# A fused adaLN attention + MLP block, forward and backward: TensorE and the SP queue in one written order, K kept on chip in the first chunk, memsets moved off GpSimd

One core of a Trainium2 chip. The metric is device time of one execution in microseconds (us), slowest core, and here there is only one. A program on one core runs "fast" or shows itself by being over 1.5% longer than the fastest run of the same kernel.

## The reference, cut to what matters

```python
def _fwd_reference(A_x, A_wqkv, A_wo, B_x, B_w1, B_b1, B_w2, B_b2, c, w_mod):   # S=2048, D=512, H=32, Dh=16, F=1792
    mod = (_silu(c) @ w_mod).reshape(c.shape[0], 6, 1, -1)
    sa, ca, ga, sb, cb, gb = ...                          # six rows of mod
    h = _layernorm(x) * (1 + ca) + sa                     # LN1
    x = x + ga * attention(h, A_wqkv, A_wo)               # softmax over all 2048 keys, 32 heads of 16
    h = _layernorm(x) * (1 + cb) + sb                     # LN2
    x = x + gb * (relu(h @ w1 + b1) ** 2 @ w2 + b2)
    return x

def reference(..., grad_out):
    out, vjp = jax.vjp(_f, ...)                           # gradients of x, weights, biases, c, w_mod
    return (out, *vjp(grad_out))
```

Ten outputs in bfloat16: the block's output and nine gradients.

## The kernel before

The program runs through these stages: an opening (LN1, first K, Q and V), forward attention over four query chunks of 512 (each 8 groups of 4 heads, two head pairs a group, 16 key blocks a pair: 256 exponential tiles a chunk), with other work woven in between as a "background" of generators; the last chunk's MLP with the weight gradients dW1 and dW2; the attention backward (16 head pairs, 16 slots of 4 tiles each); a tail. Short names: PV is the product of the exponentials with V, dS the gradient of the scores, which one DMA transpose a slot turns for the product that follows. In chunk 0 the background is the K, Q and V projections, in later chunks the MLP of the chunk before.

A scheduler places the instructions of each engine's queue, unless an engine is named in `manual_schedule`: then that engine's instructions stay in the order in which the program text emits them ("written order"). In the kernel before only TensorE is so named, in three regions. The SP engine here issues DMAs alone: loads, stores and DMA transposes.

```python
        def load_k(g):                                   # K of a group: back from DRAM
            t = kp.tile([P, S], BF16, name="KTq")
            nc.gpsimd.dma_start(t[:], self.KTq_d[g])
            return t
...
        with tc.manual_schedule(engines={mybir.EngineType.PE}):
            first = self.gen_open(Vaug, KT, QTm, stp)
            next(first)
            for n, (qc, g, jp) in enumerate(order):
                if (qc, g, jp) == (1, 0, 0):
                    bg.drain()                           # all that is left of Q, K, V is emitted here
                    self.close_qkv()
                    self.open_mlp()
                    bg.add(self.gen_weights())
...
    def gen_open(self, Vaug, KT, QTm, stp):              # (cut)
        for s4 in range(0, ST, 4):
            nc.sync.dma_start(x0[:, s4:s4 + 4, :], x_v[:, s4:s4 + 4, :])
        for t in (1, 0):
            nc.gpsimd.memset(wpads[t][:], 0.0)
...
            if s4 == 0:                                  # at the end of LN1's first block
                nc.gpsimd.dma_start(self.wmod[:, :, 2 * D:6 * D], wmod_v[:, :, 2 * D:6 * D])
...
    def gen_qkv(self):                                   # (cut) background of chunk 0
        for g in range(1, NQ):
            for s0 in range(0, S, 512):
                yield from self.gen_fm(self.mps, 1, g, s0)       # K
            yield from self.gen_fm(self.mps, 0, g, 0)            # Q of chunk 0
            yield (g, 0)
        for g in range(NQ):
            for s0 in range(512, S, 512):
                yield from self.gen_fm(self.mps, 0, g, s0)       # Q of the other chunks
        for s0 in range(0, ST, 4):                               # V transposed, for the backward
            vT = self.qkv_eb.tile([P, NQ, 4 * P], BF16, name="vT", bufs=1)
            for k in range(4):
                vp = self.vpads[k % 2]
                ...                                              # two GpSimd copies into vp
                nc.sync.dma_start_transpose(vT[:, :, k * P:(k + 1) * P], vp[:].rearrange("p g j e -> p (g j e)"))
            nc.gpsimd.dma_start(self.VTq_d.rearrange("g p s -> p g s")[:, :, s0 * P:(s0 + 4) * P], vT[:])
            yield 0
...
    def gen_weights(self):                               # (cut) background at the start of chunk 1
        nc.sync.dma_start(wo[:], ...)
        nc.sync.dma_start(w1[:], ...)
        nc.sync.dma_start(w2[:], ...)
        nc.sync.dma_start(b1r[:], ...)
        ...
        nc.sync.dma_start_transpose(self.wogaT[:] ..., wo[:] ...)
        yield ("wait", 8)
        pb = self.mps.tile([P, 1024], BF16, name="pps")
        nc.tensor.transpose(pb[:, :FT], b1r[:], self.ident[:FT, :FT])     # TensorE meets b1 here
        ...
        nc.sync.dma_start_transpose(self.W1mT[:] ..., w1[:] ...)
        nc.sync.dma_start_transpose(self.W2gbT[:] ..., w2[:] ...)
...
    def gen_mlp(self, sc, O_b):                          # (cut) comes after gen_weights in the background
        nc.sync.dma_start_transpose(OT[:] ..., O_b[:] ...)
        nc.sync.dma_start_transpose(gT[:], io["grad_out"][0, s0:s0 + 512, :])
        yield ("wait", 7)
        ...                                              # wo product, LN2
        nc.sync.dma_start_transpose(xhT[:] ..., xh[:] ...)
...
    def attn_bwd(self):                                  # (cut) one slot = G = 4 tiles
                        for c in range(SC):
                            for ib0 in range(0, ST, G):
                                if pieces and (c or ib0):
                                    nc.sync.dma_start(*pieces.pop(0))     # loads of the next group / pair
                                ...                                        # 4 tiles: scores, exp, dP, dS
                                nc.sync.dma_start_transpose(dsT[:], dsg[:].rearrange("p i a k -> p (i a k)"))
```

`pair_pieces` and `load_group` make 15 loads a group, 2.9 MB: four of 0.5 MB together during its first pair (for its own second pair), eleven of 2.4 MB during its second (for the next group). Each dS transpose moves 128 x 4096 bfloat16 numbers, 1 MB.

The softmax here doesn't subtract the row's maximum and nothing guards it: scores larger than these inputs give would overflow.

## Time and profile before

| stretch of the profiled run | length, us | what it is |
|---|---|---|
| start to first exponential | 56.5 | LN1, first K, Q, V |
| forward chunk 0 | 296.1 | attention, Q/K/V projections beside it |
| forward chunk 1 | 247.5 | attention, weights and MLP of chunk 0 beside it |
| forward chunk 2 | 250.3 | attention, MLP of chunk 1 |
| forward chunk 3, to its last exponential | 249.5 | attention, MLP of chunk 2 |
| to first exponential of the backward | 220.5 | last MLP chunk, dW1, dW2 |
| backward, first to last exponential | 1484.0 | |
| tail | 190.9 | |

The chunk borders are the starts of the 257th, 513th and 769th forward exponential. 1024 exponentials of 0.934 us make 239 us a chunk, so what a chunk takes beyond 239 is ScalarE standing. The median of three runs was 2989.28 us (2985.57 to 2990.15). The lines of the profile are in the prediction.

### The profile page before, as it was taken

How to read it: one execution, taken by the hardware profiler on the slowest of the kernel's cores; microseconds unless marked ns; L12 is line 12 of the kernel's file. 1: busy time of each engine (PE TensorE's matmuls, PEld its weight loads, DVE VectorE, ACT ScalarE, POOL GpSimd, SP SyncE). 2: the span in 40 equal slices, each digit the busy share in tenths (PEclk: the TensorE clock that was granted, in tenths of full speed). 3: DMA queues.
4: the chain of work that ended last, by engine and by line, in shares of the span. 5: the costliest groups of instructions: out<-in, count | busy, mean ns of one | idle time of the engine just before them, and what ended most of it. 6: DMA issues, size and time to landing. Idle time of an engine off the chain costs nothing. (4 is left out here: it accounts for less than half of the span.)

```text
span 2995.3 us, 72543 instructions
## 1 busy us (share of the span) xinstructions
PE 2714.6 (91%) x29931; PEld 1413.4 (47%) x30431; DVE 1799.5 (60%) x2728; ACT 2245.3 (75%) x3380; POOL 368.3 (12%) x617
## 2 busy tenths in 40 slices
PE   4699889999999988799999999999999999999796
PEld 2355445545555544744444444444444444444343
DVE  5222223322322244658888888888888888888475
ACT  3599999999999974227777777777777777777443
POOL 6233211210221132340000000000000000000000
PEclk9899999999999999999999999999999999999898
DMA  6645722330431257979999999999999999999942
GB/s 176 170 115 130 150 51 85 94 92 20 126 96 42 90 151 165 201 161 191 186 209 189 205 194 191 205 191 201 199 188 208 187 204 198 187 191 179 223 136 62
DMA packets 1304924, 467.13 MB, mean 156 GB/s; under 512 B 1235310, under 2 KB 1268592, under 8 KB 1304592
## 3 DMA queue, kind: packets, MB, share of 16 engines
q1 hardware_dynamic: 1274256, 374.68, 67.4%
q0 software_dynamic: 28224, 85.16, 9.7%
q8 instruction: 238, 3.90, 0.5%
q10 hardware_dynamic: 2112, 2.62, 0.3%
q14 instruction: 94, 0.77, 0.1%
HBM read 85.40 MB, written 67.11 MB: 51 GB/s over the span
## 5 line engine op out<-in xcount | busy, mean ns | idle before, releaser
L1189 ACT ACTIVATE pu<-st 128x512 bf16<-128x512 f32 x2048 | 1132.7, 597 | 354.5 <-PE st L1187 298.8
L1194 DVE TENSOR_TENSOR ds<-dp,pu 128x1024 bf16<-128x1024 f32 x1024 | 1208.6, 1219 | 233.9 <-ACT pu L1189 226.0
L327 ACT ACTIVATE pu<-st 128x1024 bf16<-128x1024 f32 x1024 | 956.4, 1046 | 88.7 <-PE st L324 81.7
L1187 PE MATMUL st<-KTm,QTq 128*128 128x512 bf16 x2048 | 779.0, 380 | 15.8 <-ACT pu L1189 11.6
L1137 PEld LDWEIGHTS <-dsT 128*128 128x128 bf16 x8192 | 486.9, 96 | 491.7 <-DMA dsT<-ds 21.4
L1190 PE MATMUL dp<-VTm,dOTq 128*128 128x512 bf16 x1779 | 673.2, 378 | 7.2 <-DVE ds L1194 5.9
L324 PE MATMUL st<-QTm,KTq 128*128 128x512 bf16 x1944 | 590.2, 380 | 50.0 <-DMA QTm<-QTq_d 17.0
L1137 PE MATMUL accq<-Kg,dsT 128*128 128x16 bf16 x8192 | 493.2, 170 | 30.2 <-DMA dsT<-ds 15.8
L289 PEld LDWEIGHTS <-pu 128*128 128x128 bf16 x8192 | 354.4, 96 | 291.9 <-issue 58.6
L289 PE MATMUL accbank<-Vaug,pu 128*128 128x17 bf16 x8192 | 358.5, 171 | 39.2 <-DVE O L297 30.8
L1117 PE MATMUL acckv<-ds,Qg 128*16 128x512 bf16 x2048 | 308.3, 381 | 1.1 <-DVE ds L1194 0.7
L1117 PE MATMUL acckv<-pu,dOg 128*16 128x512 bf16 x2048 | 308.3, 381 | 0.0
L1187 PEld LDWEIGHTS <-QTq 128*128 128x128 bf16 x2048 | 196.1, 96 | 223.1 <-issue 218.4
L324 PEld LDWEIGHTS <-KTq 128*128 128x128 bf16 x2048 | 194.0, 96 | 212.1 <-issue 164.3
L1190 PEld LDWEIGHTS <-dOTq 128*128 128x128 bf16 x2048 | 197.4, 96 | 38.2 <-DVE ds L1194 16.2
L1045 POOL DMA_DIRECT2D wqkv<-in_A_wqkv_dram x1 | 0.8, 791 | 1495.9 <-DMA dsT<-ds 1495.9
L450 DVE CAST ev_fm<-pps 128x512 bf16<-128x512 f32 x60 | 41.5, 692 | 139.5 <-PE pps L441 90.1
L296 DVE RECIPROCAL rl<-accbank 128x4 f32<-128x4 f32 x128 | 23.0, 180 | 165.1 <-PE accbank L289 165.0
L272 POOL DMA_DIRECT2D QTm<-QTq_d x126 | 63.8, 510 | 390.0 <-PE st L324 389.7
L914 DVE TENSOR_SCALAR rT<-pps,bias 128x512 bf16<-128x512 f32 x42 | 31.5, 751 | 117.4 <-PE pps L911 117.3
L441 PE MATMUL pps<-xm1T,wpad 128*128 128x512 bf16 x217 | 78.2, 401 | 6.7 <-DVE ev_fm L450 5.6
L922 DVE SCALAR_TENSOR_TENSOR auT<-pps,rT 128x512 bf16<-128x512 f32 x42 | 29.1, 692 | 85.4 <-PE pps L920 70.3
(308 smaller groups left out, 2112.8 us busy)
## 6 DMA issues: line engine op xcount, KB each, us to landing
KTq<-KTq_d POOLq DMA_DIRECT2D x31, 512.0 KB, 3.8
duT_d<-auT POOLq DMA_DIRECT2D x4, 1792.0 KB, 8.2
aT_d<-rT POOLq DMA_DIRECT2D x4, 1792.0 KB, 13.3
QTq_d<-ev_fm SPq DMA_DIRECT2D x32, 128.0 KB, 1.9
VTq_d<-vT POOLq DMA_DIRECT2D x4, 1024.0 KB, 6.1
O_d<-O POOLq DMA_DIRECT2D x4, 1024.0 KB, 5.5
QTq<-QTq_d SPq DMA_DIRECT2D x16, 256.0 KB, 3.8
dOTq<-dOTq_d SPq DMA_DIRECT2D x16, 256.0 KB, 3.8
```

What stands on the lines that cost most here:

```text
L272: nc.gpsimd.dma_start(QTm[j][32 * j:32 * j + 32, :], self.QTq_d[g, 32 * j:32 * j + 32, 512 * qc:512 * (qc + 1)])
L289: nc.tensor.matmul(acc[:, a, sub, :], lhsT=pu[:, a, sub * P:(sub + 1) * P], rhs=Vaug[:, kb, h, :], start=(kb == 0 and a == 0 and sub == 0) ...
L324: nc.tensor.matmul(stt[:, a, :], lhsT=KT[:, kb * P:(kb + 1) * P], rhs=QTm[2 * jp + a][:], start=True, stop=True)
L327: nc.scalar.activation(pu[:], stt[:], ACT.Exp, scale=self.scale)
L441: nc.tensor.matmul(pt[:], lhsT=self.wpads[t][:, kt, g, :], rhs=self.xm1T[:, kt, s0:s0 + 512], start=(kt == 0), stop=(kt == DT - 1))
L450: nc.vector.tensor_copy(dst, pt[:])
L1117: nc.tensor.matmul(acckv[r:r + DH, :], lhsT=T[n][:, ib, col:col + DH], rhs=src[:, a, :], start=(ib == 0), stop=(ib == ST - 1))
L1137: nc.tensor.matmul(accq[:, ib, a, :], lhsT=dsT[:, (i * 2 + a) * 4 + sub, :], rhs=T["K"][:, 4 * c + sub, col:col + DH], start=(c == 0 and i ...
L1187: nc.tensor.matmul(stt[:], lhsT=T["QT"][:, q], rhs=masked["KT"][2 * jp + a][:, c0:c0 + 512], start=True, stop=True)
L1189: nc.scalar.activation(pu[:, a, :], stt[:], ACT.Exp, scale=self.scale)
L1190: nc.tensor.matmul(dp[:, a, :], lhsT=T["dOT"][:, q], rhs=masked["VT"][2 * jp + a][:, c0:c0 + 512], start=True, stop=True)
L1194: nc.vector.tensor_tensor(dsg[:, i], dp[:], pu[:], ALU.mult)
```

## The change

Its intent: no hoisting into the SP queue. SP joins TensorE in the written order, from LN1 to the end of the backward; the text is rearranged so that this order is a good one. K of the next group stays in SBUF in chunk 0, memsets and element work leave GpSimd, the first PV product of a group is held back by one tile more, and the stage of weight gradients gets its loads in written places.

```diff
-        phases = [self.phase0, self.phase_fwd, self.phase5, self.phase6]
-        for ph in phases:
-            ph()
+        self.phase0()
+        with tc.manual_schedule(engines={mybir.EngineType.PE, mybir.EngineType.SP}):
+            self.phase_fwd()
+            self.phase5()
+        self.load_tail()
+        self.phase6()
 ...
-        pup = self.open_pool("fwp", bufs=4)
+        pup = self.open_pool("fwp", bufs=5)
 ...
-            nc.gpsimd.memset(t[:], 0.0)                     # QTm; likewise wpads, Vaug
+            nc.vector.memset(t[:], 0.0)
 ...
-        def load_k(g):
+        def load_k(qc, g):
+            if qc == 0:
+                return self.KT_next
 ...
-                    if len(pend) > 2:
+                if len(pend) > (3 if pend[0][3] == 0 else 2):
+                    pv(pend.pop(0))
+                    if len(pend) > 2 and pend[0][3] > 2:
                         pv(pend.pop(0))
 ...
-                    nc.gpsimd.tensor_scalar(xhat1[:, st, :], ...)
+                    nc.vector.tensor_scalar(xhat1[:, st, :], ...)
 ...
-            for s0 in range(0, S, 512):
-                yield from self.gen_fm(self.mps, 1, g, s0)
+            while self.cur_g < g - 1:
+                yield ("wait", 0)
+            KT = self.KT_next = kp.tile([P, S], BF16, name="KTq")
             yield from self.gen_fm(self.mps, 0, g, 0)
             yield (g, 0)
+            for s0 in range(0, S, 512):
+                yield from self.gen_fm(self.mps, 1, g, s0, dst=KT[:, s0:s0 + 512])
+            yield (-g, 0)
 ...
-        while fill.mark != "half":
-            fill.next()
+        fill.until("dw1")
+        next(g2)
+        fill.until("half")
         self.load_bwd()
```

Cut: the transposes of an LN1 block before their evacuations, half of V's copies to ScalarE, tile names shared so that memory suffices, the bias sum in another PSUM pool, and the backward's loop, which only loses one level of indentation. V's transposes, the weights' loads and the backward's loads stand where they stood.

## The prediction

> **What bounds the kernel now.** I first cut the span into stages, at the first exponential tile, the start of the second query chunk, the end of the forward attention, the start and the end of the attention backward. Columns: stretch, its length, then busy time with instruction counts for PE, PEld, DVE, ACT and POOL, then granted clock, DMA share, GB/s.
>
> ```profile
> 0.00:56.50 56.50, 18.12 (x109) 9.21 (x112) 32.96 (x71) 13.78 (x20) 43.86 (x53) 0.97 0.62 180
> 56.50:351.40 294.90, 244.00 (x2832) 135.88 (x2881) 73.90 (x160) 242.39 (x259) 94.37 (x195) 0.94 0.60 138
> 351.40:1104.00 752.60, 695.42 (x8348) 385.10 (x8499) 227.67 (x674) 716.90 (x770) 142.13 (x245) 0.99 0.32 82
> 1104.00:1318.00 214.00, 185.62 (x1538) 115.40 (x1547) 110.10 (x449) 62.83 (x152) 79.06 (x114) 0.95 0.83 196
> 1318.00:2807.00 1489.00, 1429.35 (x16264) 699.67 (x16534) 1254.38 (x1104) 1147.08 (x2078) 1.52 (x2) 1.00 1.09 194
> ```
>
> Forward attention is ScalarE's: 1024 exponentials took 956.4 us (the groups table), 0.934 us each, so 239 us a chunk. The first chunk takes 294.9 us with 52.5 us of ScalarE idle (294.9 - 242.4); the other three hold 35.7 us of it. The last forward chunk with the weight gradients (214 us) and the backward (half of the run) are TensorE's: TensorE's gaps there add up to about 30 and 41 us in the waits. So what the change can win is bounded by the opening, the 52.5 us, some of the 35.7, some of the 30, and a few of the 41.
>
> Next, the order of time shows what made the idle time. In the opening:
>
> ```profile
> 12.96 6.95 POOL L370 MEMSET wpad<- 128x4096 bf16 x2
> 13.65 8.92 DVE L214 TENSOR_SCALAR opcaT<-modT 128x4 f32<-128x4 f32 x1
> 19.86 2.25 POOL L375 MEMSET Vaug<- 128x512 bf16 x1
> 32.90 1.52 ACT L396 ACTIVATE xhat<-x,nmr,rstd 128x512 bf16<-128x512 bf16 x2 [14.22 <-DVE nmr L390]
> ```
>
> A VectorE instruction on 128x4 numbers takes 8.92 us; it ends when GpSimd's memsets end (22.1). LN1's first output comes at 32.9, though x had landed at 9.3. In chunk 0 the large hole, and the SP queue ahead of it:
>
> ```profile
> 86.77 0.57 SPq L824 DMA_DIRECT2D wo<-in_A_wo_dram  x1
> 92.84 0.59 SPq L825 DMA_DIRECT2D w<-in_B_w_dram  x1
> 104.93 4.07 SPq L481 DMA_TRANSPOSE vT<-vpad  x2
> 109.09 0.53 SPq L451 DMA_DIRECT2D KTq_d<-ev_fm  x1
> 131.82 1.02 ACT L327 ACTIVATE pu<-st 128x1024 bf16<-128x1024 f32 x1 [22.40 <-PE st L324]
> ```
>
> SP is a single queue, and the scheduler hoisted work into it that is needed 250 us later (V transposes, MLP weights) ahead of the K and Q stores that the next group waits for: TensorE lost 17 us to the Q load, ScalarE 22.4. The same happens to the weight gradients, where loads of the backward's second group stand between the transposed dU blocks:
>
> ```profile
> 1225.31 0.32 SPq L1169 DMA_DIRECT2D Kg<-ktm_d  x1
> 1225.72 5.50 SPq L731 DMA_TRANSPOSE du_blk<-duT_d  x1
> 1238.66 6.45 PE L748 MATMUL dps<-du_blk,xh 128*128 128x128 bf16 x64 [5.60 <-DMA du_blk<-duT_d]
> ```
>
> **What the Trainium skill says.** "SBUF — State Buffer", section Who interferes with whom: VectorE's fast two-port modes and GpSimd take one shared port pair by an exclusive lock for a whole instruction. The trace agrees (8.92 us, ended by the memsets). "VectorE: DVE Perf Modes", section Zero memsets can be issued as uint32: a zero memset of bf16 costs half its elements. The trace agrees: the backward's zero memsets of 128x2048 bf16 appear as 128x1024 uint32, 912 ns each; so 128x4096 is an estimated 1.8 us. "TensorE: Matmul & The Clock Gate", Part 1: the array halves its clock after about 3.4 us idle. Here 512-column matmuls start 0.43 us apart after a hole (40 us) and 0.215 us when busy. "DMA: Bandwidth & Descriptors", section Queues, rings and completion order: each DMA engine consumes a queue's descriptors in ring order; I use it for a small load behind large ones, which this trace does not test.
>
> **The change part by part.**
>
> 1. Memsets, pads and LN1. With the memsets on VectorE (two of 1.8 us plus small ones, in its idle time before x lands), the statistics run through: 9.3 + 4 x 0.65 + aggregation and small ones 1 + GpSimd power 1.05 + 0.4 gives LN1 output at about 15. The wqkv loads, issued from 6.3 with a median of 10.4 us to land, then set the pace: K weights at about 16.5, four ScalarE copies of 0.54, first K matmul near 19-20 instead of 39. ScalarE has about 3-4 us more copies before the first exponential. First exponential at about 40 instead of 56.6: **-16 us**.
>
> 2. Transposes of a block before their evacuations: now each of four rounds waits about 1.1 us for the one before (59.5 to 63.7); after, 1.6 us of transposes and 1 us to the first evacuation. About 2 us on each of the two blocks inside chunk 0: **-4 us**.
>
> 3. Chunk 0 without hoisted work on SP, K kept on chip (no store-and-load of K between projection and use): the 22.4 us hole and its cold restart (2.5 us) go, and the 4.4 us at 340 where VectorE scaled w2 while the PV accumulator waited: **-29 us**.
>
> 4. The first PV product of a group held back by one more tile: TensorE waited 30.8 us, 58 times, for the accumulator; ScalarE feels about ten of these at 0.5 to 2 us in the later chunks: **-8 us**.
>
> 5. SP's written order at the chunk boundary, the price. The count of background steps puts the 16 V transposes at step 4 of group 7 of chunk 0, 28 tiles x 0.934 = 26 us before chunk 1. They run two at a time through two padding buffers and one result buffer: a transpose lands after 3 to 5 us, four take 8.6, then a store of 0.9 to issue and 6.1 to land before the next four: about 15 us a round, which the trace shows as stores at 62.4, 79.0, 96.6 and 116.7. So SP is held for 3 x 15 + 7 = 52 us, until 26 us after chunk 1 starts. Only behind them stand the loads of wo, w1, w2 (4.1 MB, an estimated 20 us at some 200 GB/s, as w2's 1.8 MB took 10.1) and b1, whose transpose TensorE meets, in its fixed order, 9.4 us after the chunk starts (351.4 and 360.85 now). b1 lands near +48: TensorE and so ScalarE stand about **+39 us**. The transposes of W1 and W2 (8.5 us of SP each) and of O (5, landing 9) then follow in line, where they were partly early before: the wo product, 17 us after b1's now, will wait about **+19 us** more.
>
> 6. Weight gradients: dU loads no longer wait behind the backward's loads, but also are no longer issued at 1147, only with the first fill matmuls (about 1181), which costs some 5 us at the start. 14 blocks at 3.85 plus the pieces between them would end near 1252 instead of 1264.5: **-12 us**. The bias sum in another PSUM pool takes two waits of about 2 us within this.
>
> 7. Backward: TensorE waits 15.8 us for transposed dS, in short waits once a group, just after bursts of three loads between two transposes on SP. Written order has one load at a time: **-6 us**. Everything else there (about 1 us at each turn of K and V) stays. The tail is unchanged.
>
> Sum: -16 - 4 - 29 - 8 - 12 - 6 = -75; part 5 gives +58; net -17, that is 2972.
>
> **The rivals.** (a) No stall in part 5: the loads get through earlier than I count, by quicker V transposes or because b1 overtakes w2. For it: the writer tuned everything else for the written order, and a hole of 40 us would be seen. Against it: the code sends wo, w1, w2 and b1 through SP after the V transposes, and nothing there was moved. Time then 2989 - 75 = 2914. (b) The opening gains little, because the wqkv loads or VectorE's longer list (memsets, eight more LN1 tiles, still ordered by the scheduler) hold LN1's first block: then -5 in part 1 and 2925 to 2983. (c) In the backward SP is the near bound: a dS transpose holds it about 5.1 us of 5.76 (92.2 us for 16), and with a load each time 5.7; written order could make TensorE wait 10 to 20 us more. In the trace 11 loads fitted with few waits, so I give it little.
>
> **Range and chances.** I give the stall 7 in 10. With it 2972, give or take 15; without it 2914, give or take 12. The point is between them, nearer the first: 2958. 8 in 10 lie in 2905 to 2988. Faster by 2% means under 2929.5: mostly rival (a), 0.29. Slower needs over 3049: 0.03.
>
> **What would show it.** First exponential near 40; no ScalarE gap over 7 us in chunk 0; a ScalarE gap of 30 to 50 us about 10 us into the second chunk, released by TensorE waiting for b1 or w1, and one near 20 us for O's transpose; dU matmuls without waits over 5 us; the stage of the backward within 10 us of 1489. No long gap at the chunk boundary makes part 5 wrong, and the time then falls to about 2914.

## The result, and the profile after

The changed kernel took 2995.54 us (median of 4 runs, 2992.25 to 2995.83); the kernel before, beside it, 2989.72 (4 runs, 2985.57 to 2993.23). The ratio is 1.0018, 95% interval 1.0000 to 1.0035: the same, within 2%. A ratio here is the mean time of one kernel's fast runs over that of the other's of the same rounds, so it is not quite the ratio of the medians quoted.

The profiled run of the changed kernel was its fastest (2992.25), that of the kernel before (2997.03) was slower than all four timed beside it, though over all later rounds 12 of this kernel's 32 timed runs were slower still (2985.57 to 3000.97). So the pair of profiles differs by -4.8 us of span where the medians differ by +5.8; those 10 us are run-to-run spread. The opening, chunks 0 and 1 differ by as much or far more; smaller differences rest on one profile of each kernel, and where other runs show their spread, it is said below.

The stages of the changed kernel, in the columns of the prediction's first fence:

```profile
0.00:46.20 46.20, 19.51 (x109) 9.39 (x112) 27.26 (x82) 17.98 (x28) 14.18 (x32) 0.93 0.59 194
46.20:301.80 255.60, 238.91 (x2848) 134.95 (x2899) 59.40 (x135) 245.09 (x264) 79.32 (x168) 1.00 0.41 102
301.80:609.50 307.70, 231.79 (x2799) 129.16 (x2847) 89.16 (x245) 238.21 (x258) 59.35 (x106) 0.89 0.44 111
609.50:1093.20 483.70, 458.61 (x5509) 253.99 (x5605) 146.37 (x433) 475.05 (x512) 92.09 (x160) 1.00 0.31 81
1093.20:1306.80 213.60, 189.80 (x1572) 117.12 (x1583) 114.39 (x467) 63.95 (x154) 83.18 (x119) 0.97 0.85 190
1306.80:2802.90 1496.10, 1430.06 (x16235) 697.49 (x16504) 1252.03 (x1101) 1147.30 (x2077) 0.00 (x0) 1.00 1.08 194
2802.90:2990.50 187.60, 142.06 (x873) 68.40 (x885) 102.61 (x275) 62.80 (x104) 7.33 (x10) 0.89 0.42 133
```

Row 3 is chunk 1: ScalarE is busy 238 us of 307.7, TensorE's granted clock falls to 0.89. Row 2, chunk 0, is nearly full: 245 of 255.6. In one table, with the kernel before, and with two of the experiments told below:

| stretch, us | before | after | difference | SP left to the scheduler (e2) | best version (e15) |
|---|---|---|---|---|---|
| to first exponential | 56.5 | 46.2 | -10.3 | 46.1 | 44.5 |
| chunk 0 | 296.1 | 255.6 | -40.5 | 263.2 | 262.3 |
| chunk 1 | 247.5 | 307.7 | +60.2 | 251.1 | 248.3 |
| chunk 2 | 250.3 | 242.4 | -7.9 | 242.5 | 240.3 |
| chunk 3 | 249.5 | 241.3 | -8.2 | 241.4 | 242.4 |
| last MLP chunk, dW1, dW2 | 220.5 | 213.6 | -6.9 | 215.6 | 216.2 |
| backward | 1484.0 | 1496.1 | +12.1 | 1487.9 | 1485.5 |
| tail | 190.9 | 187.6 | -3.3 | 189.6 | 189.9 |
| span | 2995.3 | 2990.5 | -4.8 | 2937.4 | 2929.4 |

The gains, -77 us, are nearly all eaten by two losses, chunk 1 and the backward.

**Chunk 1.** The SP queue in order of time at the chunk boundary (start, duration, instruction, count):

```profile
294.24 39.98 SPq L495 DMA_TRANSPOSE vT<-vpad  x12
334.26 0.58 SPq L844 DMA_DIRECT2D wo<-in_A_wo_dram  x1
334.89 0.53 SPq L845 DMA_DIRECT2D w<-in_B_w_dram  x1
346.21 0.37 SPq L846 DMA_DIRECT2D w<-in_B_w_dram  x1
346.68 0.91 SPq L851 DMA_DIRECT2D dxT<-in_B_b_dram  x1
...
366.14 8.38 SPq L873 DMA_TRANSPOSE W1mT<-w  x1
374.61 9.17 SPq L877 DMA_TRANSPOSE W2gbT<-w  x1
383.83 2.04 SPq L899 DMA_TRANSPOSE fT<-O_b  x1
```

and ScalarE beside it, with the idle time in front of a tile in brackets and what ended it:

```profile
358.56 1.02 ACT L332 ACTIVATE pu<-st 128x1024 bf16<-128x1024 f32 x1 [47.39 <-PE pps L861]
...
391.04 1.02 ACT L332 ACTIVATE pu<-st 128x1024 bf16<-128x1024 f32 x1 [14.69 <-PE st L329]
```

The V transposes hold SP until 334; the second w2 load (346.21) then waits 11 us for the memory of V's last result to come free; b1 follows it, and TensorE's b1 transpose (L861), which is ahead of the scores in the written order, waits 46.7 us for it. Of these, 10 pass after b1 was issued: TensorE goes on at 356.9, just after the w2 load issued ahead of b1 had landed (356.0). A small load behind a large one is what the prediction said that its own trace did not test. The second gap is the wo product waiting for O's transpose, which stands behind W1's and W2's.

**The opening.** Three engines' timelines of the changed kernel:

```profile
1.30 0.91 POOL L432 DMA_DIRECT2D wmod<-in_w_mod_dram  x1 [0.35 <-issue]
...
1.25 9.88 SPq L373 DMA_DIRECT2D x<-in_A_x_dram  x4
...
15.04 0.69 DVE L394 BATCH_NORM_STATS2 stats<-x 128x6 f32<-128x512 bf16 x1 [1.99 <-DMA x<-in_A_x_dram]
```

GpSimd has nothing left to do at the start, so the scheduler (GpSimd is not in the written order) pulls wmod's 2 MB load, written behind LN1's first block, to 1.30 us. Its 2 MB are then under way beside x, and the statistics of x, which wait for it, start at 15.04 instead of 9.29. The VectorE memsets of 128x4096 bf16 took 1.76 us each as 128x2048 uint32, against the prediction's estimate of 1.8.

**The backward.** SP in the kernel before, and then in the changed one, at the same stage:

```profile
1688.84 1.03 SPq L1169 DMA_DIRECT2D KTm<-KTq_d  x2
1689.97 5.40 SPq L1201 DMA_TRANSPOSE dsT<-ds  x1
1695.42 1.04 SPq L1169 DMA_DIRECT2D VTm<-VTq_d  x2
1696.50 0.42 SPq L1169 DMA_DIRECT2D QTq<-QTq_d  x1
```

```profile
1639.42 5.12 SPq L1224 DMA_TRANSPOSE dsT<-ds  x1
1644.59 0.57 SPq L1192 DMA_DIRECT2D Kg<-ktm_d  x1
1645.25 6.11 SPq L1224 DMA_TRANSPOSE dsT<-ds  x1
1651.42 0.58 SPq L1192 DMA_DIRECT2D Qg<-qtm_d  x1
```

One load stands before each transpose now, two or three stood before some. In the changed kernel's lines SP goes from one to the next without a pause (each starts within 0.1 us of the end of the one before). TensorE's waits for transposed dS (total us, times, longest), before and after, in the same window of the backward:

```profile
PE accq L1137 <- DMA dsT<-ds: 10.8, 9, 2.0
```

```profile
PE accq L1161 <- DMA dsT<-ds: 19.8, 22, 1.8
```

The times between successive turns of K and V (the finished gradients of K and V of a head pair are transposed there, so it is a clock of the backward) say where: an interval without loads of a next group takes 92.2 us in both kernels, 5.76 us a slot. Those with them took 1.5 to 2.7 us more before, six of them, 12.5 us in all; after, 2.3 to 5.8 more, seven of them, 25.3 in all. The seventh is there because group 1's loads, which the scheduler had sent during the weight gradients, now run inside the backward. These two profiles are the extremes of their kinds: over all runs with these two orders (the table that ends the experiments) the written order has 1493.9 us in the mean of five profiles and the scheduler's 1487.0 of six, so the order costs about 7 us rather than 12.

### The profile page after: what moved, and what is told of

Read it like the earlier page. It is cut to its first block, busy times and chain, and to the rows that moved or that the text cites. A ratio compares the mean times of both kernels' runs of the same rounds, so it can differ in the third digit from the quotient of the medians.

```text
span 2990.5 us, 72431 instructions
## 1 busy us (share of the span) xinstructions
PE 2710.8 (91%) x29931; PEld 1410.5 (47%) x30431; DVE 1791.2 (60%) x2735; ACT 2250.4 (75%) x3392; POOL 335.4 (11%) x591
## 5 line engine op out<-in xcount | busy, mean ns | idle before, releaser
L332 ACT ACTIVATE pu<-st 128x1024 bf16<-128x1024 f32 x1024 | 953.9, 1049 | 81.6 <-PE pps L861 47.4
L294 PEld LDWEIGHTS <-pu 128*128 128x128 bf16 x8192 | 345.0, 96 | 239.9 <-issue 14.7
L294 PE MATMUL accbank<-Vaug,pu 128*128 128x17 bf16 x8192 | 349.0, 171 | 12.3 <-DVE O L302 4.1
L934 DVE TENSOR_SCALAR rT<-pps,bias 128x512 bf16<-128x512 f32 x42 | 31.5, 751 | 111.9 <-PE pps L931 111.4
L767 PE MATMUL dps<-du_blk,xh 128*128 128x128 bf16 x896 | 56.5, 226 | 13.5 <-DVE junk L782 7.6
```

The source lines that it names most:

```text
L294: nc.tensor.matmul(acc[:, a, sub, :], lhsT=pu[:, a, sub * P:(sub + 1) * P], rhs=Vaug[:, kb, h, :], start=(kb == 0 and a == 0 and sub == 0) ...
L332: nc.scalar.activation(pu[:], stt[:], ACT.Exp, scale=self.scale)
L767: nc.tensor.matmul(g4[:, kt, :], lhsT=xh2[:, st, kt * P:(kt + 1) * P], rhs=du[:, st, :], start=(st == 0), stop=(st == ST - 1))
```

## The experiments

All ran with three timed rounds beside the kernel before of the same rounds, and all were correct except one. Ratios are to the kernel before; the changed kernel's is 1.0018. First exponential, gaps and stage lengths are from each run's own profile.

**V's transposes early (e1).** One round of four in each of groups 1 to 4 of chunk 0:

```diff
             if 2 <= g <= 5:
+                yield from self.gen_v(4 * (g - 2))      # the loop body over s0, moved into a generator
...
-        for s0 in range(0, ST, 4):
-            vT = ...
```

> The changed kernel with the V transposes written earlier: one round of four in each of groups 1 to 4 of the first chunk, instead of all sixteen at the start of group 7. Nothing else is moved. Theory (the SP queue is held by the V transposes and their stores when the second chunk starts, and w2's memory is released only by the last V store): the 47.4 us ScalarE gap in front of the second chunk shrinks to 3 to 20 us, the 14.7 us gap behind it stays near 15, and the time falls by 28 to 45 us against the changed kernel, to 2950 to 2967. Rival (the gap is the loads' own time, or the bias transpose waits for something else): the gap stays over 35 us and the time stays within 10 us of 2995.

2953.26 us (2950.93 to 2959.61), ratio 0.9872 [0.9857, 0.9887]. ScalarE and SP in this run:

```profile
350.82 1.02 ACT L332 ACTIVATE pu<-st 128x1024 bf16<-128x1024 f32 x1 [14.59 <-PE st L329]
...
285.25 0.57 SPq L850 DMA_DIRECT2D wo<-in_A_wo_dram  x1
...
294.66 1.10 SPq L857 DMA_DIRECT2D dxT<-in_B_b_dram  x1
```

The 47 us gap is gone altogether, more than the 3 to 20 us left that I had expected: SP reaches wo at 285 instead of 334 and b1 at 295 instead of 347. The 14.6 us gap is untouched, as it has another cause. So the place of the V transposes (and of the stores behind them) in the queue made the first gap. Moving them is not free: chunk 0 takes 262.7 us instead of 255.6, with a ScalarE gap of 4.2 us at 156 us.

**SP back to the scheduler (e2)**, all else of the change kept:

```diff
-        with tc.manual_schedule(engines={mybir.EngineType.PE, mybir.EngineType.SP}):
+        with tc.manual_schedule(engines={mybir.EngineType.PE}):
```

> The changed kernel with only TensorE in written order; SP's order is left to the scheduler everywhere. Theory (written SP order costs the boundary gap and about 12 us of the backward, and saves the hole of the first chunk): no gap over 20 us at the start of the second chunk, the backward from its first to its last exponential near 1484 us instead of 1496, and either a new hole in the first chunk (then near 2970) or none, because K stays on chip (then 2930 to 2950). Rival (written order of SP is not what costs): within 10 us of 2995 with the same gaps.

2938.12 us (2935.27 to 2940.53), ratio 0.9818 [0.9803, 0.9832]: 2% under the changed kernel. In its SP queue

```profile
56.47 1.23 SPq L495 DMA_TRANSPOSE vT<-vpad  x1
...
62.83 0.38 SPq L844 DMA_DIRECT2D wo<-in_A_wo_dram  x1
```

the scheduler hoists V transposes and weights to 60 us as it did before, yet the 22 us hole that this made in the kernel before is not there: the longest gap in chunk 0 is 4.9 us. In the changed text K no longer has to go through that queue before its use, which is the likely reason. So the hoisting, which the change set out to end, did little harm beside the rest of the change, and the SP order costs: of the 53 us between the two spans, chunk 1 holds 56.6 and the backward 8.2, and chunk 0 gives back 7.6 (the table above).

**SP in written order in the forward part only (e3)** (nested regions, so that SP's ends with the forward):

```diff
-        with tc.manual_schedule(engines={mybir.EngineType.PE, mybir.EngineType.SP}):
-            self.phase_fwd()
+        with tc.manual_schedule(engines={mybir.EngineType.PE}):
+            with tc.manual_schedule(engines={mybir.EngineType.SP}):
+                self.phase_fwd()
             self.phase5()
```

> The changed kernel with SP in written order up to the end of the weight gradients only; in the backward SP's order is the scheduler's again, TensorE's stays written. Theory (one load in front of each transposed dS makes SP late): waits of TensorE for dS fall from 25 us to about 15, first to last exponential of the backward from 1496 to about 1484 to 1487, total 9 to 12 us less than the changed kernel. Rival (the backward's extra time is the clock, the chip or the place of the first group's loads): less than 4 us.

2986.77 us (2986.13 to 2992.86), ratio 0.9980 [0.9963, 0.9996]; backward 1489.7, above the expected 1484 to 1487, both gaps of the boundary unchanged (46.0 and 14.1). Half of the profiled backward's loss comes back.

**The rest of wmod by SP in its written place (e4)**:

```diff
-                nc.gpsimd.dma_start(self.wmod[:, :, 2 * D:6 * D], wmod_v[:, :, 2 * D:6 * D])
+                nc.sync.dma_start(self.wmod[:, :, 2 * D:6 * D], wmod_v[:, :, 2 * D:6 * D])
```

> The changed kernel with the 2 MB load of the rest of w_mod on the SP queue, at its written place behind LN1's first block, instead of on GpSimd's queue, where it now goes out at 1.3 us. Theory (freed of its memsets GpSimd sends this load ahead of x, so that x lands at 15.0 instead of 9.3 us): x lands near 9 to 10, the first exponential comes at 40 to 43 us instead of 46.2, total 3 to 6 us less. Rival (the wqkv weights set the first block's pace anyway): first exponential within 1.5 us of 46.2.

2992.77 us (2989.91 to 2993.77), ratio 0.9999 [0.9984, 1.0014]. First exponential 44.3, not 40 to 43: SP issues x in 4.56 us again instead of 9.88, but VectorE starts the statistics at 12.84. x is no longer what it waits for. The scheduler put memsets (two of 1.76 us) and the short chain for silu(c) ahead of it, and among them VectorE idles 1.68 us for which the trace names no cause. So the hoisted load was a part of the shortfall, and VectorE's longer list (rival b of the prediction) is likely another.

**The backward's loads from GpSimd (e5)**:

```diff
-                                nc.sync.dma_start(*pieces.pop(0))
+                                nc.gpsimd.dma_start(*pieces.pop(0))
```

> The changed kernel, but the backward's per-group loads are issued by GpSimd instead of SP, at the same written places. Theory (SP has no room for a load in every slot of 5.76 us, of which a dS transpose holds it for 5.1): the backward, first to last exponential, falls from 1496 to 1478-1488 us, intervals between turns of K and V are all near 92-93 us, TensorE's waits for transposed dS fall from 24.8 us to under 12, and the run is 9 to 18 us shorter than the changed kernel (ratio to the kernel before about 0.996). Rival (the order of TensorE, or traffic in the DMA engines wherever the loads are issued): the backward stays at 1493 or more. The 47 and 15 us gaps at the chunk boundary stay.

3037.65 us (3031.26 to 3049.83), ratio 1.0145 [1.0117, 1.0173]; backward 1528.6. The theory missed. The rival's mark (1493 or more) is met, but by 35 us too much, as the experiment did not isolate what it meant to. GpSimd's queue is not tied to SP's, and it sent a group's loads at once:

```profile
1686.59 1.02 POOL L1192 DMA_DIRECT2D KTm<-KTq_d  x2 [90.22 <-PE st L1210]
1687.60 0.97 POOL L1192 DMA_DIRECT2D VTm<-VTq_d  x2
1688.56 1.11 POOL L1192 DMA_DIRECT2D QTq<-QTq_d  x2
1689.66 1.06 POOL L1192 DMA_DIRECT2D dOTq<-dOTq_d  x2
```

and in TensorE's waits

```profile
PE accq L1161 <- DMA dsT<-ds: 44.5, 6, 9.3
```

Six waits of up to 9.3 us: a dS transpose in flight with the whole group's loads lands late, and the loads themselves take 14.7 us to land in the median (dOTq), where SP's took 3.8. SP, which issues nothing but transposes here, is held up too:

```profile
1688.82 35.35 SPq L1224 DMA_TRANSPOSE dsT<-ds  x4
```

Four transposes take 35 us, where 5 us each is usual. What it does show: loads that another engine issues also make a transpose on SP longer, so it is not only the time in which SP issues loads that counts.

**Up to three loads per slot (e6)**, on SP, in written order:

```diff
-                                nc.sync.dma_start(*pieces.pop(0))
+                                for _ in range(min(3, len(pieces))):
+                                    nc.sync.dma_start(*pieces.pop(0))
```

> The changed kernel, but up to three loads per slot between two dS transposes in the backward instead of one, on SP still. If it is the spreading that costs (every slot is filled by one load and none recovers): the backward falls to 1484-1491 us, as in the kernel before, dS waits to about 16-20 us. If it is only that group 1's loads now run inside the backward, or the number of loads: it stays at 1494-1498. If the scheduler's freedom in other things was what the kernel before had: also 1494-1498.

3001.79 us (3001.50 to 3010.04), ratio 1.0027 [1.0009, 1.0046]; backward 1503.6, over all the expected ranges. Worse than one at a time: spreading is not what costs.

**O's transposes early (e7)**, ahead of W1's and W2's on SP:

```diff
-                bg.add(self.gen_mlp(qc, self.take_o(qc, O32)))
+                m = self.gen_mlp(qc, self.take_o(qc, O32))
+                if qc == 0:
+                    next(m)                  # emits the two transposes now
+                bg.add(m)
```

> The changed kernel, but the transposes of O and of the output gradient for the first MLP chunk are written as soon as O is complete, ahead of the transposes of W1 and W2 on SP. Theory of the second gap (the O transpose stands in the SP queue behind 17.5 us of weight transposes): the 14.7 us gap falls under 2 us, the 47 us gap stays within 2 us, and the run is 12 to 15 us shorter than the changed kernel, ratio about 0.997. Rival (O's transpose is late for its own input or slow by itself, or the first MLP products then wait for something else, W1mT, W2gbT): a gap of 8 us or more comes back within the next 60 us.

2981.74 us (2980.49 to 2983.41), ratio 0.9954 [0.9939, 0.9969], 14 us under the changed kernel. The 14.7 us gap is gone, the first stays (46.7), and none over 4.7 comes after. The second gap was a matter of queue order alone.

**Four repairs at once (e9)**: V early, O early, wmod by SP, the backward's loads from GpSimd.

> The written order kept for both engines, with four repairs at once: V's transposes written one round each into groups 1 to 4 of the first chunk, O's transposes ahead of W1's and W2's, the last two thirds of wmod loaded by SP in its written place, the backward's loads issued by GpSimd. If the three places found are all that the written order loses: 2953 (V early alone) less 13 (O) less 10 (backward) less 2 = 2928, range 2918-2938, no ScalarE gap over 5 us at the chunk boundary, ratio about 0.979. That would be at or below the variant with SP left to the scheduler (2938). If it stays over 2940, the written order has a cost that I haven't found.

2988.21 us (2986.25 to 2994.14), ratio 0.9980 [0.9960, 1.0000]: far over the expected 2928. The forward is as expected (last exponential at 1043.3 instead of 1093.2); the backward takes 1526.7, like the other run with loads from GpSimd, and in dW2 TensorE waits 15.9 us for a load. The loads from GpSimd are the likely fault: both runs that have them lose over 30 us in the backward, and without them (next run) the loss is gone.

**The same without that repair (e8)**: V early, O early, wmod by SP, SP in the backward left to the scheduler.

> Written order for TensorE throughout and for SP in the forward part only; V's transposes early, O's transposes ahead of W1's and W2's, the rest of wmod by SP in its written place; SP in the backward left to the scheduler, its loads on SP. From the runs so far: V early alone 2953, less 13 for O, less 7 to 11 for the backward, less 2 for wmod: 2930, range 2922-2940, ratio about 0.979. No ScalarE gap over 9 us at the chunk boundary. If it is below 2935 it beats the variant in which SP is left to the scheduler throughout (2938), and written order in the forward part pays once its three places are mended; if it is above 2938, it doesn't.

2940.89 us (2935.01 to 2947.20), ratio 0.9814 [0.9795, 0.9832], 0.9 us over the expected range; backward 1487.4. By the mark that I had set (over 2938) the written order in the forward doesn't pay yet. One gap is left at the boundary, over the 9 us that I had allowed (ScalarE, then SP):

```profile
359.41 1.02 ACT L336 ACTIVATE pu<-st 128x1024 bf16<-128x1024 f32 x1 [10.35 <-PE st L333]
...
323.89 8.82 SPq L883 DMA_TRANSPOSE W1mT<-w  x1
332.75 9.08 SPq L887 DMA_TRANSPOSE W2gbT<-w  x1
343.43 8.41 SPq L934 DMA_TRANSPOSE fT<-xh  x1
```

TensorE waits 9.4 us for LN2's transpose (fT from xh, L934), which stands behind W2's.

**No loads in the backward (e10)** after group 0's, whose data is used again (the error is in the gradients of x and wqkv). Its output is wrong, which doesn't matter for the time.

```diff
-                        pieces = self.pair_pieces(g, 1)
+                        pieces = self.pair_pieces(g, 1) if g == 0 else []
...
-                        Tn, pieces = self.load_group(g + 1)
-                        pieces = self.pair_pieces(g + 1, 0) + pieces
+                        Tn, pieces = T, []
```

> The changed kernel with the backward's loads after group 0's left out and group 0's data used again (wrong dq, dk, dv on purpose). The DMA engines are over 100% busy in the backward, so a load's data must come out of the time of the dS transposes. If the loads are all that stretches the slow intervals: every interval between turns of K and V is within 1 us of 92.2, TensorE's waits for transposed dS fall under 3 us, and the backward falls from 1496 to 1470-1476, the run 20 to 26 us shorter than the changed kernel. If TensorE's or SP's own order is part of it: the backward stays over 1482.

2969.36 us (2968.43 to 2970.37), ratio 0.9909 [0.9893, 0.9926]; backward 1471.0. Every interval takes 92.2 us (the last, 90.1 in every kernel), and TensorE waits for dS once, at the end:

```profile
PE accq L1161 <- DMA dsT<-ds: 5.0, 1, 5.0
```

So the loads are all of the 25 us. The stretch view of the same 92.2 us (last two columns: DMA share, GB/s), here and, with loads, in the changed kernel:

```profile
1407.00:1499.20 92.20, 89.24 (x1024) 43.98 (x1040) 78.41 (x70) 71.75 (x130) 0.00 (x0) 1.00 1.02 184
```

```profile
1407.00:1499.20 92.20, 87.23 (x997) 42.45 (x1013) 76.40 (x68) 69.86 (x128) 0.00 (x0) 1.00 1.14 207
```

With no loads at all the share is 1.02, at 184 GB/s, nearly all of it dS transposes (16 of 1 MB in 92.2 us are 182 GB/s). That does not mean that the engines are full, as the expectation took it: the share adds up the times of packets, which overlap (up to 30 at once on the 16 engines, counted from this trace's packets), and with loads the engines moved 207 GB/s in the same stretch. What the trace does show is SP's queue. Its dS transposes (durations in ns, lowest, median, highest, then first and last start), without loads and then in the changed kernel during the eleven loads of a second pair:

```profile
L1223 SPq DMA_TRANSPOSE dsT<-ds x19: 4776/5297/5433, 1595.3 to 1699.1; - x19
```

```profile
L1224 SPq DMA_TRANSPOSE dsT<-ds x12: 4792/5452/6110, 1591.5 to 1658.4; - x12
```

Without loads one starts every 5.77 us, which is TensorE's pace. With a load before each, one starts every 6.08 us, though SP never pauses: 5.45 for the transpose in the mean, 0.57 for the load, the rest between them. Counted so for the seven stretches of eleven loads, a slot takes 5.99 to 6.29 us; times eleven, less 5.76 each, that is 2.6 to 5.8 us (29 in all), against the 2.3 to 5.8 (25 in all) by which these intervals are longer, and the stretch with the most is the longest interval too. So SP falls behind by its own queue. The four loads of a first pair make it late too, but for four slots only, and those intervals take 92.2 us in every kernel. Why a transpose is longer beside a load (5.24 to 5.55 us in these stretches, 5.06 in the mean without loads) is not shown by this run, which takes away the issuing and the data at once; the run with loads from GpSimd points to the data.

**The written order alone (e11)**, put on the kernel before:

```diff
-        with tc.manual_schedule(engines={mybir.EngineType.PE}):        # in all three regions
+        with tc.manual_schedule(engines={mybir.EngineType.PE, mybir.EngineType.SP}):
```

> The kernel before with one part of the change alone: SP joins TensorE in the written order in the three regions that had it. My account: +62 at the chunk boundary, +12 in the backward, -25 in the first chunk (no hole), -12 in the weight gradients: 3030, ratio 1.012, range 1.005 to 1.020. Rival (the written order needs the rest of the change to work, as K still goes through DRAM between projection and use): new ScalarE holes over 10 us in the first chunk, ratio over 1.02. If the order is no loss by itself: ratio 1.003 or less.

3024.27 us (3023.37 to 3026.34), ratio 1.0093 [1.0078, 1.0108], in the range. The boundary's gaps are 36.4 and 12.7 us (49 instead of 62), the backward 1491.3 (+7 instead of +12), and no hole over 6.9 us in chunk 0, which takes 271.5 us instead of 296. So SP's order by itself gains 24.5 us in chunk 0, and is a loss over the whole run without the rest of the change too.

**The opening alone (e12)**, put on the kernel before: memsets, pads, LN1's odd tiles and half of V's copies off GpSimd.

> The kernel before with the memsets, pads, LN1's odd tiles and half of V's copies moved off GpSimd, nothing else. My account of the opening: first exponential at 44-47 instead of 56.6 (x late behind the hoisted load of wmod, as in the changed kernel), the run 8 to 11 us shorter, ratio 0.997. Rival (the scheduler, with GpSimd free earlier, hoists more into SP and the hole of the first chunk grows): first exponential as said, but ratio 1.000 or more, holes over 25 us in the first chunk.

2974.46 us (2973.99 to 2983.20), ratio 0.9932 [0.9916, 0.9949]. First exponential 47.0 as said, with wmod again sent at 1.30 us; the hole of chunk 0 is 17.6 us instead of 22.4, and chunk 0 is 5.6 us shorter. The profiles differ by -14 us, the ratio says -20: the profiled run was the slowest of its four (2983.20, the others within 0.6 us of 2974).

**Two loads per slot, from a pair's first slot (e13):**

```diff
-                            if pieces and (c or ib0):
-                                nc.sync.dma_start(*pieces.pop(0))
+                            for _ in range(min(2, len(pieces))):
+                                nc.sync.dma_start(*pieces.pop(0))
```

> The changed kernel, the backward's loads on SP in written order, but two per slot and from the first slot of a pair, as near as the written order comes to where the scheduler put them (it issued them about two slots earlier, at the turn of K and V, where TensorE stands anyway). With no loads the backward is 1471.0; the changed kernel pays 25 for 7 groups (3.6 each), the scheduler's order about 2.6 to 2.8 for 6. If the place is what matters: 1484-1489. If it is only that group 1's loads run inside the backward and any place costs the same: 1493-1497. If pairs are worse as threes were: 1498-1504.

2999.97 us (2999.25 to 3006.75), ratio 1.0020 [0.9999, 1.0041]; backward 1498.4, at the low end of the third expectation (pairs are worse). The earlier place wins nothing.

**V early, O early, W1's and W2's transposes behind LN2's, wmod by SP (e14)**, with the loads of the run above. The new part:

```diff
         nc.sync.dma_start_transpose(xhT[:] ..., xh[:] ...)
+        if sc == 0:
+            nc.sync.dma_start_transpose(self.W1mT[:] ..., self.w1[:] ...)
+            nc.sync.dma_start_transpose(self.W2gbT[:] ..., self.w2[:] ...)
```

> Written order for both engines throughout, with V's transposes early, O's transposes early, the transposes of W1 and W2 behind the first transpose of LN2's output (the 10 us gap left over in the run before stood behind them), wmod by SP in its written place, and the backward's loads as in the run above. Theory of the left-over gap (LN2's transpose lands late because W2's is in the DMA engines ahead of it): no ScalarE gap over 4 us from 160 us to 420 us; last forward exponential at about 1034 instead of 1043.5. Time 2928 to 2936 if the backward is 1487, ratio 0.979; 2936-2942 if the loads' place changes nothing. Rival (the stand moves on to W2's transpose): a gap of 5 us or more between 360 and 480 us.

2947.41 us (2938.80 to 2948.62), ratio 0.9833 [0.9813, 0.9852]. At the boundary no gap over 2.2 us is left, so the theory of that gap holds; the forward ends at 1041.4, not at 1034, as chunk 0 has a gap of 5.5 us of its own; the backward takes 1500.7, like the run above with the same loads, so the time is over both expected ranges.

**The same with SP in the backward left to the scheduler (e15).**

> As the run above, but SP in the backward left to the scheduler with single loads. Forward as above; backward 1487 as in the earlier run with this order. Time 2928-2934, ratio 0.978: 7 to 12 us under the same kernel with W1's and W2's transposes ahead. If it is not under 2936, the gap at 359 us was not on the path.

2931.14 us (2926.44 to 2939.26), ratio 0.9787 [0.9766, 0.9808], as expected. LN2's transpose now goes ahead of the weights', and the gap shrinks from 10.35 to 3.02 us:

```profile
352.66 1.02 ACT L336 ACTIVATE pu<-st 128x1024 bf16<-128x1024 f32 x1 [3.02 <-PE st L333]
...
344.02 2.09 SPq L932 DMA_TRANSPOSE fT<-xh  x1
346.15 10.82 SPq L934 DMA_TRANSPOSE W1mT<-w  x1
357.01 9.07 SPq L935 DMA_TRANSPOSE W2gbT<-w  x1
```

This is 2.1% under the kernel before (the interval, 1.9 to 2.3%, leaves open whether it is a full 2%), and further under the changed kernel. Against SP left to the scheduler throughout (0.9818) the intervals overlap: the mended written order in the forward is at least as good, and it isn't shown to be better.

The backward under the orders tried, in one place:

| SP order in the backward | first to last exponential, us |
|---|---|
| no loads | 1471.0 |
| scheduler (before, e2, e3, e8, e12, e15) | 1484.0 to 1489.7 |
| written, one load per slot (after, e1, e4, e7, e11) | 1491.3 to 1496.1 |
| written, two per slot from the first (e13, e14) | 1498.4, 1500.7 |
| written, three per slot (e6) | 1503.6 |
| loads from GpSimd (e5, e9) | 1528.6, 1526.7 |

## Why the prediction was wrong

| part | predicted | profiled pair |
|---|---|---|
| 1 opening | -16 | -10.3 |
| 2, 3 chunk 0 | -33 | -40.5 |
| 4 PV held back, later chunks | -8 | -16.1 (chunks 2 and 3) |
| 5 chunk boundary | +58 | +60.2 (chunk 1) |
| 6 weight gradients | -12 | -6.9 |
| 7 backward | -6 | +12.1 |
| tail | 0 | -3.3 |
| sum | -17 | -4.8 |

The measured 2995.54 lies above the range (2905 to 2988) and 37.5 us above the point.

**Part 7 failed in its sign, and with it rival (c) was dismissed wrongly.** The prediction read "short waits ... just after bursts of three loads" as the harm of bursts, expected -6 from spreading, and set rival (c), 10 to 20 us more waiting, aside with "In the trace 11 loads fitted with few waits, so I give it little". Measured: +12.1 in the profiled pair, about +7 over all runs. (Of the 15.8 us of waits that it hoped to shorten, 5.0 are a single wait at the end that no order removed.) Spread loads are the best of the written orders (1491.3 to 1496.1, against 1498.4 for pairs and 1503.6 for threes), so the observation on bursts was right, but it isn't the main thing. Rival (c) had the sign, about the size, and the place: SP is the near bound. It had counted 5.7 us a slot with a load, just inside the 5.76. Measured are 6.0 to 6.3, as beside loads the transpose takes 5.24 to 5.55 us instead of 5.1, and 0.17 us are lost between the two; eleven such slots make up the 2.3 to 5.8 us of each slow interval (the run without loads, e10, has the counting). Two parts make up the loss: a seventh group of loads in the stage, and a higher price per group, 3.6 against 2.1 us in the profiled pair, 3.3 against 2.7 over all runs with either order (each measured from the 1471.0 without loads). Why the scheduler's order pays less per group stays open: placing the loads earlier or in pairs did not bring it down, and its own runs differ (3.1 per group in the run with SP written in the forward only, 2.4 in the best version).

**Part 5 was right, and the point moved away from it.** 39 + 19 were predicted, with gaps of 47.4 and 14.7 us; the sum, 58 against 62, fits, and the two repairs (V early, O early) each removed exactly its own gap. The first was longer by a link that the working did not have: the w2 load waiting 11 us for memory that V's last store held, ahead of b1. The second was shorter. The V transposes held SP for 56 us, not 52 (277.9 to 334.3 us in the changed kernel). The rounds of "about 15 us" were not what the cited stores show (62.4, 79.0, 96.6, 116.7 are 17 to 20 apart), but in the changed kernel they took 14.6, 18.7 and 14.3. The weight of 3 in 10 for "no stall" (rival a) pulled the point from 2972 to 2958: 14 of the 37.5 us. That rival's main argument was that the writer would have seen such a hole; what was in the code, that the loads stand behind the V transposes and nothing there was moved, was the better evidence.

**Part 1 was mis-sized**, -10.3 for -16. The statistics start at 15.04 instead of 9.3, because freeing GpSimd lets the scheduler send wmod's 2 MB beside x. The prediction had not asked what the freed queue will do first. Taking that away gives 2 us (44.3 instead of 46.2); the rest is, as far as shown, VectorE's longer list, rival (b), which was priced at more (-5 in place of -16) than it cost.

**Part 6 was mis-sized**, -6.9 for -12. The profile shows TensorE waiting 7.6 us for VectorE in dW1, where it waited 4.1 for it before: with the loads out of the way VectorE's work per block sets the pace in places. How much is SP's order is not shown: by itself (e11) the order brings this stretch from 220.5 to 210.5, yet with SP left to the scheduler the rest of the change (e2) has 215.6.

**Parts 2 to 4 were low** by 15 us together, which hid some of the rest. They were not run one by one. Chunk 0 gains 40.5 us in all, 33 with SP left to the scheduler, 24.5 with SP's order alone, 5.6 with the opening alone. So the parts overlap: the 22 us hole goes either by ordering SP or, as is likely, by keeping K on chip. Chunks 2 and 3 gain 8 us each with SP in either order, and at most 1.8 with the opening alone; that the held-back PV product does it is likely, and only argued.

The prediction was for medians; what remains, some 10 us between the profiled pair's -4.8 and the medians' +5.8, is the spread of single runs.

## What to carry to other kernels

An order fixed for one queue must be checked link by link at each phase border: here 16 V transposes, needed a millisecond later, stood in front of loads that TensorE needed 10 us later, and moving either of two pieces of text was worth 1.5% and 0.6%. Ask first whether the thing that hoisting hurt can be taken out of the queue; with K kept on chip the scheduler's hoisting left no gap over 5 us in that chunk. Where one queue holds a transfer in nearly every slot (here SP, 5.1 of 5.76 us), add up the slot with everything in it, with durations measured beside other traffic, and take a DMA share near 1 neither for room nor for the lack of it. When an engine is relieved, look at what its queue will then send early.

## What the Trainium skill lacked or had wrong

- "Advanced Engine Details and Errata", section X-Bar Transpose (TRN2), says that transpose DMAs are as fast as regular ones and expects 350 to 400 GB/s; "DMA: Bandwidth & Descriptors", section Latency and other measured facts, gives 261 GB/s for a non-contiguous case. Here the changed kernel's SP sent transposes of 128 x 4096 bfloat16 numbers from SBUF to SBUF back to back, with no loads beside them, from 1664.3 to 1685.4 us, and the engines moved 200 GB/s. Whether SP's 5.1 us for each or the engines set this rate is not shown.
- No page read gives a figure for loads from GpSimd beside a stream of transposes. Here 256 KB loads landed in 3.3 to 3.8 us (QTq, dOTq) when SP sent them one at a time and in 8.6 and 14.7 us when GpSimd sent them together; the backward was 32 us longer. This run does not separate the queue from the bunching.
- Nor does one say what a scheduler does with a queue that has been relieved, or how to check a queue's written order at a phase border; here these were worth about 6 us (the statistics of x starting at 15.04 instead of 9.29) and 62 us.
